# The last batch's tail rows are stored in two transfers instead of four

## The chip, the cores and the metric

The kernel runs on one core of a Trainium2 chip. The core has TensorE (PE in the profile), VectorE (DVE), ScalarE (ACT), GpSimd (POOL) and SyncE (SP), and 16 DMA engines that move data between the chip's memory and the core. A transfer is issued by an instruction on SP, ACT or POOL and then runs by itself. The metric is the device time of one execution in microseconds (us); shorter is better.

## The reference, cut to what matters

Eight batches of 576 rows go through sliding-window attention with 8 heads of 64, and then through a token mix and a channel mix:

```python
scores = scale * np.matmul(q, k.transpose(0, 1, 3, 2))     # 8 batches, 8 heads, 576 x 64
scores = np.where(mask, scores + bias[None], -1000000000.0) # window of 128, slope per head
attn = np.exp(scores - np.max(scores, axis=-1, keepdims=True))
x = np.matmul(attn / np.sum(attn, axis=-1, keepdims=True), v)   # -> 8 x 576 x 512
...
h = np.maximum(xt @ w_tok1, 0.0) @ w_tok2                   # token mix, 576 -> 256 -> 576
u = x + h.transpose(0, 2, 1)
h2 = np.maximum(u @ w_ch1, 0.0) @ w_ch2                     # channel mix, 512 -> 1536 -> 512
return (u + h2).astype(np.float32)                          # 8 x 576 x 512
```

## The kernel before, in words

The 576 rows of a batch are four blocks of 128 rows and a tail of 64. Two batches form a pair, and their two tails share one block: batch `2 * pr` in partitions 0 to 63, batch `2 * pr + 1` in partitions 64 to 127. The code calls this block `TAIL`. It is worked on with the second batch of the pair, so the output rows of the last tail block belong to batches 6 and 7 and are computed with batch 7, the last one.

The whole program is first written down as a list of operations with costs and ranks (`plan.op`), a planner (`Plan.run`) simulates them with those costs and settles the order of each engine, and `Plan.emit` writes the instructions in that order. Each operation holds a small function that issues its instructions when it is emitted. The planner's costs don't come from the instructions but are given by hand: the store of a tail block is planned as an operation of SP with cost 550.

For each batch, `side` computes attention and token mix, and `main` the channel mix. The first channel product is in `main` and its helpers; the second, of the four full blocks, is in `second` (lines 1160 to 1256), where the 512 x 512 results are formed by seven products of quarter size, whose sums are added in VectorE (L1202) and stored as quarters of 2 blocks x 128 rows x 256 columns (L1214). The last of these quarters in the last batch is formed by `last_product` in two blocks (matmuls L1263, add L1267); its two stores go out on SP and on ACT (L1270).

The tail block's second product is at the end of `main`: 12 matmuls (L1133), an add of the residual in VectorE (L1140), and a store (L1150). In the last batch it is cut into two column halves of 256 (`cuts`), each with matmuls, add and store of its own, and its stores go out on SP (`q_` is `nc.sync`). The outputs wait in a ring of six buffers, `ob` (named raw and ob in the profile). At the end of the program SP waits until the transfers have landed (L1350).

The order of SP's stores at the end of the program is: one quarter of L1214; the first column half of the tail; two quarters of L1214; the second column half of the tail; the L1270 store of one block. ACT issues the other L1270 store. A store in DRAM terms: the rows of `out` are 512 floats, of which a store of 256 columns writes 1 KB each; a batch is 576 rows.

Of the kernel before, what the change touches and what calls it, by code (L numbers as in the profile page):

```python
# [382 lines left out]
def kernel(  # L383
# [16 lines left out]
    P = nc.NUM_PARTITIONS  # L400
    B, H, S, D = q.shape
# [4 lines left out]
    NC = S // P  # L406
    R = S - NC * P
    NB = 2 * NC + 1
    TAIL = 2 * NC
# [24 lines left out]
    def bank(choice=ONE):  # L434
        return plan.buf("ps", choice)
# [581 lines left out]
    def main(b, rank):  # L1017
        pr, half = b // 2, b % 2
# [5 lines left out]
        if b == 0:  # L1024
            first = [bank() for _ in range(PIECES)]
            for blk in blocks:
                for t, ct in enumerate(first):
                    def go(t=t, ct=ct, blk=blk):
                        for cb in range(NCB):
                            pe_.matmul(ct()[:, blk * P : (blk + 1) * P], lhsT=WC1[:, cb, t * P : (t + 1) * P],  # L1030
                                       rhs=uT()[:, cb, blk * P : (blk + 1) * P],
                                       start=cb == 0, stop=cb == NCB - 1)
# [89 lines left out]
        for blk in blocks:  # L1122
            cuts = [slice(0, DM)]
            if b == B - 1 and blk == blocks[-1]:
                cuts = [slice(0, DM // 2), slice(DM // 2, DM)]
            for cols in cuts:
                o2 = bank()
                n = cols.stop - cols.start
                for g in range(NHT // 3):
                    def go(blk=blk, g=g, o2=o2, cols=cols):  # L1130
                        for t in range(3 * g, 3 * g + 3):
                            l = r2t()[:, t, :] if blk == TAIL else r2()[:, t, (blk % NC) * P : (blk % NC + 1) * P]
                            pe_.matmul(o2()[:, cols], lhsT=l, rhs=WC2[:, t, cols], start=t == 0, stop=t == NHT - 1)  # L1133

                    rk = rank(648)
                    rd = [(r2t, g * 3 // 4), (r2t, (g * 3 + 2) // 4)] if blk == TAIL else [(r2, t) for t in range(3 * g, 3 * g + 3)]
                    plan.op("PE", 649 * n / DM, go, rk, reads=rd, needs=lc2[3 * g : 3 * g + 3],
                            **({"makes": o2} if g == 0 else {"adds": o2}))
                ob = plan.buf("ob")
                plan.op("DVE", 160 + 530 * n / DM, lambda blk=blk, o2=o2, ob=ob, cols=cols: dve_.tensor_tensor(  # L1140
                    out=ob()[:, cols], in0=o2()[:, cols], in1=ub()[:, blk, cols], op=ALU.add), rk, makes=ob, uses=[o2],
                    reads=[(ub, blk)])

                late = b >= FROM_P and blk not in blocks[-2:] or FROM_P <= b < B - 1
                q_ = nc.gpsimd if late else nc.sync

                def store(blk=blk, ob=ob, cols=cols, q_=q_):
                    if blk == TAIL:
                        for i in range(2):
                            q_.dma_start(out=out[2 * pr + i, NC * P : S, cols], in_=ob()[i * R : (i + 1) * R, cols])  # L1150
                    else:
                        q_.dma_start(out=out[b, (blk % NC) * P : (blk % NC + 1) * P, cols], in_=ob()[:, cols])

                if late:
                    plan.dma(store, P, -1, uses=ob)
                else:
                    plan.op("SP", 550, store, rk, uses=[ob])
# [197 lines left out]
```

## Time and profile before

| what | value |
|---|---|
| timed runs | 277.51, 278.48, 278.57 us; median 278.48 |
| the profiled execution's own time | 277.36 us |
| its span | 275.6 us, at a granted TensorE clock of 1.0 |
| TensorE busy | 268.4 us (97%) |
| VectorE busy | 210.3 us (76%) |
| bytes moved by DMA | 38.71 MB |

The span runs from the first to the last instruction of the profiled execution; the execution's own time is a little longer. A row of the timeline gives start, length, engine, line and operation (output <- input), and in brackets how long the engine had been idle and what ended that. The letters SPq and ACTq mark instructions that issue a transfer: their length is that of the issue, not of the transfer. The DMA view gives the packets of each queue, the time they took as a share of 16 engines' time in the stretch asked for, and, for each line that issues, the median time from issue to landing. q1 is the queue of SP's transfers, q10 that of ACT's, q0 that of GpSimd's; q8 and q14 fetch instructions. A table by stretches has columns for stretch, length, busy time of PE, PEld, DVE, ACT and POOL with the number of instructions, the granted clock, the mean busy share of the 16 DMA engines, and GB/s.

### The profile page before, as it was taken

How to read it: one execution, taken by the hardware profiler on the slowest of the kernel's cores; microseconds unless marked ns; L12 is line 12 of the kernel's file. 1: busy time of each engine (PE TensorE's matmuls, PEld its weight loads, DVE VectorE, ACT ScalarE, POOL GpSimd, SP SyncE). 2: the span in 40 equal slices, each digit the busy share in tenths (PEclk: the TensorE clock that was granted, in tenths of full speed). 3: DMA queues.
4: the chain of work that ended last, by engine and by line, in shares of the span. 5: the costliest groups of instructions: out<-in, count | busy, mean ns of one | idle time of the engine just before them, and what ended most of it. 6: DMA issues, size and time to landing. Idle time of an engine off the chain costs nothing.

```text
span 275.6 us, 6968 instructions
## 1 busy us (share of the span) xinstructions
PE 268.4 (97%) x2790; PEld 180.8 (66%) x2824; DVE 210.3 (76%) x496; ACT 139.1 (50%) x239; POOL 114.0 (41%) x144
## 2 busy tenths in 40 slices
PE   8999999999999999999999999999999999999994
PEld 4665655676676556585658655576676655599983
DVE  7596799987898379956979468763998459967983
ACT  5475893426940388109950187116960089106560
POOL 8898747940454039700891009600462410021000
PEclk9999999999999999999999999999999999999999
DMA  8999999999899899979999859999599760043014
GB/s 156 154 165 178 179 200 183 155 129 210 127 107 130 176 233 142 152 120 193 189 149 148 199 146 95 135 158 242 68 99 126 195 132 0 2 113 137 1 49 145
DMA packets 167553, 38.71 MB, mean 140 GB/s; under 512 B 155808, under 2 KB 166688, under 8 KB 167520
## 3 DMA queue, kind: packets, MB, share of 16 engines
q0 software_dynamic: 114032, 19.77, 91.8%
q1 hardware_dynamic: 51264, 17.83, 33.4%
q10 hardware_dynamic: 2224, 0.66, 1.2%
q8 instruction: 22, 0.36, 0.5%
q14 instruction: 11, 0.09, 0.1%
HBM read 35.85 MB, written 9.44 MB: 164 GB/s over the span
## 4 chain that ended last, share of the span: by engine, by line
PE 81%; DMA 6%; DVE 5%; POOL 4%; issue 2%; SPq 1%; POOLq 0%
PE ps L1234 25%; PE ps L1045 24%; PE ps L760 6%; PE ps L693 5%; DMA qk<-in_k_dram 5%; PE ps L805 4%; PE ps L848 4%; PE ps L1088 4%; PE ps L967 3%; PE ps L1133 3%; DVE pe L726 2%; POOL qk L530 2%; POOL v L530 1%; DMA uT<-ub 1%; PE ps L815 1%
## 5 line engine op out<-in xcount | busy, mean ns | idle before, releaser
L1045 PE MATMUL ps<-uT,WC 128*128 128x512 bf16 x306 | 77.9, 379 | 1.3 <-DMA uT<-ub 0.2
L716 ACT ACTIVATE pe<-ps 128x1024 bf16<-128x1024 f32 (+1 forms) x76 | 63.4, 890 | 19.1 <-PE ps L693 18.8
L530 POOL DMA_DIRECT2D v<-in_v_dram x40 | 34.1, 858 | 91.8 <-PE ps L760 88.6
L1051 ACT ACTIVATE r<-ps 128x512 bf16<-128x512 f32 x77 | 45.0, 604 | 51.4 <-PE ps L1045 49.3
L1045 PEld LDWEIGHTS <-WC 128*128 128x128 bf16 x328 | 29.1, 98 | 29.3 <-issue 0.9
L726 DVE TENSOR_TENSOR pe<-pe,mask 128x1024 bf16<-128x1024 bf16 (+1 forms) x64 | 38.7, 609 | 12.0 <-ACT pe L716 11.5
L1234 PEld LDWEIGHTS <-r 128*128 128x128 bf16 x372 | 36.1, 98 | 7.3
L530 POOL DMA_DIRECT2D qk<-in_k_dram x38 | 33.0, 876 | 4.6 <-DMA WC<-in_moe_w_ch_dram 2.4
L530 POOL DMA_DIRECT2D qk<-in_q_dram x38 | 32.7, 866 | 1.7 <-PE ps L1234 0.7
L1234 PEld LDWEIGHTS <-s 128*128 128x128 bf16 x288 | 27.4, 98 | 6.0 <-issue 2.0
L776 DVE TENSOR_TENSOR xb<-ps,rt 128x256 bf16<-128x256 f32 (+1 forms) x72 | 28.9, 417 | 0.8
L760 PEld LDWEIGHTS <-pe 128*128 128x128 bf16 (+1 forms) x560 | 22.6, 98 | 9.1 <-DVE pe L726 1.3
L760 PE MATMUL ps<-v,pe 128*128 128x65 bf16 (+1 forms) x560 | 26.9, 194 | 0.3
L1234 PE MATMUL ps<-WC,r 128*128 128x256 bf16 x192 | 25.4, 273 | 0.0
L1234 PE MATMUL ps<-WT,s 128*128 128x256 bf16 x192 | 24.8, 273 | 0.0
L866 DVE TENSOR_TENSOR ub<-ps,xb 128x512 bf16<-128x512 f32 x34 | 21.3, 683 | 2.5 <-PE ps L848 2.5
L1234 PE MATMUL ps<-WT,r 128*128 128x256 bf16 x180 | 22.3, 273 | 0.0
L693 PEld LDWEIGHTS <-qkT 64*128 64x128 bf16 x560 | 14.8, 94 | 10.7 <-issue 8.2
L1202 DVE TENSOR_TENSOR raw<-ps,ub 128x512 f32<-128x512 f32 x22 | 15.0, 686 | 8.1 <-PE ps L1234 8.1
L693 PE MATMUL ps<-qkT 64*128 64x128 bf16 (+1 forms) x304 | 19.5, 216 | 0.0
L1093 ACT ACTIVATE r2t<-ps 128x512 bf16<-128x512 f32 x12 | 7.2, 600 | 22.9 <-PE ps L1088 22.7
L773 DVE RECIPROCAL rt<-ps 128x4 f32<-128x4 f32 (+1 forms) x76 | 12.6, 176 | 7.3 <-PE ps L760 6.9
(101 smaller groups left out, 348.1 us busy)
## 6 DMA issues: line engine op xcount, KB each, us to landing
out_dram<-raw SPq DMA_DIRECT2D x18, 256.0 KB, 2.8
v<-in_v_dram POOLq DMA_DIRECT2D x32, 128.0 KB, 5.1
qk<-in_k_dram POOLq DMA_DIRECT2D x30, 128.0 KB, 5.5
qk<-in_q_dram POOLq DMA_DIRECT2D x30, 128.0 KB, 5.1
WC<-in_moe_w_ch_dram POOLq DMA_DIRECT2D x8, 384.0 KB, 9.4
out_dram<-ob SPq DMA_DIRECT2D x5, 256.0 KB, 2.6
out_dram<-ob POOLq DMA_DIRECT2D x4, 256.0 KB, 2.7
out_dram<-raw POOLq DMA_DIRECT2D x4, 256.0 KB, 2.9
```

Of the source, the lines that this page charges most:

```text
L530: nc.gpsimd.dma_start(out=to()[p0 : p0 + n, :, :], in_=rows(src, b, s0, n))
L693: pe_.matmul(wide(e)[:, i, kind, a:z], lhsT=ts[kb]()[e * D : (e + 1) * D, NHP + i, :], rhs=ts[blk]()[e * D : (e + 1) * D, i, a:z], start=n ...
L716: act_.activation(out=pb()[:, e, :, lo:, c0:c1_], in_=wide(e)[:, :, lo:, c0:c1_], func=ACT.Exp, scale=scale)
L726: dve_.tensor_tensor(out=o, in0=o, in1=heads(mk, es), op=ALU.mult)
L760: pe_.matmul(view()[a:z, at, i, :], lhsT=pb()[:, e, i, kind, a:z], rhs=vb()[:, h, 0 : D + 1], start=m == 0, stop=m == len(mms) - 1, skip_g ...
L773: dve_.reciprocal(out=rt()[r0:r1_, 0:n, :, :], in_=view()[r0:r1_, :, :, D : D + 1])
L776: dve_.tensor_tensor(out=x4(), in0=view()[r0:r1_, :, :, 0:D], in1=rt()[r0:r1_, 0:n, :, :].broadcast_to([r1_ - r0, n, 4, D]), op=ALU.mult)
L866: plan.op("DVE", 690, lambda blk=blk, ht=ht, hs=hs: dve_.tensor_tensor(out=ub()[:, blk, :], in0=ht()[:, hs], in1=xb()[:, blk, :], op=ALU.a ...
L1045: pe_.matmul(ct()[:, :], lhsT=WC1[:, cb, t * P : (t + 1) * P], rhs=uT()[:, cb, :], start=cb == 0, stop=cb == NCB - 1)
L1051: plan.op("ACT", 600, lambda t=t, ct=ct: act_.activation(out=r2()[:, t, :], in_=ct()[:, :], func=ACT.Relu), rk, part=(r2, t), uses=[ct], o ...
L1202: dve_.tensor_tensor(out=v, in0=both(bk), in1=src, op=ALU.add)
L1234: pe_.matmul(of(bk, c), lhsT=l(t, c), rhs=w(t), start=first, stop=g == 1 and t == HK - 1, skip_group_check=True)
```

## The change

In the last batch, each column half of the tail block is stored by one transfer that covers both batches' 64 rows, instead of by one transfer for each batch. The source is all 128 partitions of the buffer; the destination takes 64 rows in each of two batches. The four transfers of the last tail block become two. The tails of the other pairs are stored as before, and the planner's cost of the store is not changed.

```diff
@@ -1145,7 +1145,9 @@
                 q_ = nc.gpsimd if late else nc.sync
 
                 def store(blk=blk, ob=ob, cols=cols, q_=q_):
-                    if blk == TAIL:
+                    if blk == TAIL and b == B - 1:
+                        q_.dma_start(out=out[2 * pr : 2 * pr + 2, NC * P : S, cols], in_=ob()[:, cols])
+                    elif blk == TAIL:
                         for i in range(2):
                             q_.dma_start(out=out[2 * pr + i, NC * P : S, cols], in_=ob()[i * R : (i + 1) * R, cols])
                     else:
```

Lines behind the change are two higher in the changed kernel: the new transfer is L1149, the two transfers of the other pairs L1152, and L1214, L1267, L1270 and L1350 become L1216, L1269, L1272 and L1352.

## The prediction

> **What bounds the kernel now.** I read the page's first lines, then the end of the chain that ended last, then the last 10 us in order of time: the change touches only stores issued there.
>
> ```profile
> span 275.6 us, 6968 instructions
> PE 268.4 (97%) x2790; PEld 180.8 (66%) x2824; DVE 210.3 (76%) x496; ACT 139.1 (50%) x239; POOL 114.0 (41%) x144
> PE 81%; DMA 6%; DVE 5%; POOL 4%; issue 2%; SPq 1%; POOLq 0%
> ...
> 270.31 1.32 PE ps L1263 x12
> 271.63 0.02 issue
> 271.66 0.42 DVE raw L1267
> ```
>
> TensorE is busy 97% of the span and makes up most of the chain. None of its work changes. The chain's last link is the VectorE add at 271.66, which ends at 272.08; the span ends at 275.6. So 3.5 us of the span come behind all computing, and they are stores. The timeline shows who issues them (SPq and ACTq rows: start, length of the issue):
>
> ```profile
> 266.75 0.42 DVE L1140 TENSOR_TENSOR ob<-ps,ub 128x256 f32<-128x256 f32 x1 [0.27 <-PE ps L1133]
> ...
> 267.24 1.12 SPq L1150 DMA_DIRECT2D out_dram<-ob  x2
> ...
> 268.06 0.69 DVE L1202 TENSOR_TENSOR raw<-ps,raw 128x512 f32<-128x512 f32 x1 [0.35 <-PE ps L1234]
> ...
> 268.77 1.69 SPq L1214 DMA_DIRECT2D out_dram<-raw  x2
> ...
> 270.35 0.42 DVE L1140 TENSOR_TENSOR ob<-ps,ub 128x256 f32<-128x256 f32 x1 [0.29 <-PE ps L1133]
> 270.84 1.11 SPq L1150 DMA_DIRECT2D out_dram<-ob  x2
> 271.00 0.42 DVE L1267 TENSOR_TENSOR raw<-ps,ub 128x256 f32<-128x256 f32 x1 [0.23 <-PE ps L1263]
> 271.66 0.42 DVE L1267 TENSOR_TENSOR raw<-ps,ub 128x256 f32<-128x256 f32 x1 [0.23 <-PE ps L1263]
> 272.04 0.56 SPq L1270 DMA_DIRECT2D out_dram<-raw  x1
> 272.12 0.36 ACTq L1270 DMA_DIRECT2D out_dram<-raw  x1
> ```
>
> The pairs at 267.24 and 270.84 (L1150) are the four transfers of the change. SP issues the last store of its own at 272.04, though its data were ready at 271.42: it stood behind the second pair. ACT's last store waits for its own add only. The DMA view of the stretch 262 to 276 gives issue to landing (last column), and the list of SP's waits what the end waits for:
>
> ```profile
> out_dram<-ob SPq DMA_DIRECT2D x4, 64.0 KB, 2.1
> out_dram<-raw SPq DMA_DIRECT2D x1, 128.0 KB, 2.2
> out_dram<-raw ACTq DMA_DIRECT2D x1, 128.0 KB, 1.8
> SPq L1350 <- DMA out_dram<-raw: 1.6, 1, 1.6
> ```
>
> SP's last store lands at 272.04 + 2.2 = 274.24, ACT's at 272.12 + 1.8 = 273.92. The end waits for the later one, and 275.6 - 274.24 = 1.36 us of ending follow. Stretches of 0.2 us show when bytes flow (last two columns: mean busy share of the 16 DMA engines, GB/s):
>
> ```profile
> 268.20:268.40 0.20, 0.20 (x4) 0.18 (x2) 0.20 (x1) 0.00 (x0) 0.00 (x0) 1.00 0.08 20
> 268.40:268.60 0.20, 0.20 (x4) 0.18 (x2) 0.20 (x1) 0.00 (x0) 0.00 (x0) 1.00 0.77 195
> ...
> 269.60:269.80 0.20, 0.20 (x4) 0.18 (x2) 0.20 (x1) 0.00 (x0) 0.00 (x0) 1.00 0.48 169
> ...
> 270.80:271.00 0.20, 0.20 (x4) 0.18 (x2) 0.00 (x0) 0.00 (x0) 0.00 (x0) 1.00 0.07 26
> 271.00:271.20 0.20, 0.20 (x4) 0.18 (x3) 0.20 (x1) 0.00 (x0) 0.00 (x0) 1.00 0.88 302
> ...
> 272.00:272.20 0.20, 0.00 (x0) 0.00 (x0) 0.08 (x1) 0.00 (x0) 0.00 (x0) 1.00 0.79 220
> ...
> 273.60:273.80 0.20, 0.00 (x0) 0.00 (x0) 0.00 (x0) 0.00 (x0) 0.00 (x0) 1.00 0.91 302
> 273.80:274.00 0.20, 0.00 (x0) 0.00 (x0) 0.00 (x0) 0.00 (x0) 0.00 (x0) 1.00 0.09 26
> ```
>
> First bytes of the first tail pair flow at about 268.35, 1.1 us behind its issue; of the two L1214 stores at about 269.7 and 270.95; of the second pair at about 271.95; the last byte flows at about 273.85. Each store is a short burst on all sixteen engines, with gaps between.
>
> **The change, part by part.** *Issues.* Two of SP's issues go, at the lengths of the first row:
>
> ```profile
> L1150 SPq DMA_DIRECT2D out_dram<-ob x6: 472/548/589, 158.3 to 271.4; - x6
> ...
> L1214 SPq DMA_DIRECT2D out_dram<-raw x18: 372/478/576, 57.2 to 270.1; - x18
> ```
>
> One issue fewer in the first pair is worth nothing: SP's next store (268.77) waits for an add that ends at 268.06 + 0.69. One fewer in the second frees SP at about 271.4, so its last store goes out at about 271.46 instead of 272.04 and lands near 273.7. Then ACT's, at 273.92, is last. The gain is 274.24 - 273.92 = 0.3 us, if nothing else changes. The new issue has three dimensions, as L1214's have, and those take 0.37 to 0.58 us; I take 0.55. Were it over 1.1 us, the gain would be gone.
>
> *Order and queues.* Planned costs are untouched, so every engine's instructions keep their order; no buffer of these stores is used again, so nobody waits for them but the end. SP's next issue waits for no transfer of the new pair. The other pairs of batches keep two transfers. Cost: none.
>
> *How the transfer is dealt out.* This is the term that decides. In all transfers of the kernel before, both sides begin with 64 or 128 rows at one stride: L1214's store puts the 128 partitions ahead of its two blocks, L1150's stores are 64 rows. The new destination begins with a count of 2, the batches, 576 rows apart, and then 64 rows; the source is 128 partitions at one stride. A cut along the first dimension of both sides can only make two shares, of 64 rows each. Sixteen shares would need a cut inside the second dimension on one side and inside the first on the other. No transfer in the trace asks for that, so no row prices it; the ends are two shares and sixteen. I take two, because each transfer the trace does show can be cut along its first dimension. The Trainium skill says the same ("DMA: Bandwidth & Descriptors", "Why a DMA increments its semaphore by 16 and not by 1"): the number of engines is the largest up to 16 that divides the slowest dimension of both sides, here 2; the trace, with sixteen throughout, agrees but doesn't test it. The same page's "Rules for kernel authors" speaks for the change: two transfers to disjoint partition halves should be one of 128 partitions. By that rule alone the sum is the -0.3 us above.
>
> *What two shares cost.* Each of two DMA engines moves 64 rows of 1 KB for each new transfer, and its part of every other store. DMA view by stretch, 264.8 to 267 (one L1214 store), 268.2 to 268.9 (one 64 KB store), 271.5 to 273 (a lone instruction packet on one engine, 0.09 MB in 11 such packets over the run, some 8 KB):
>
> ```profile
> q1 hardware_dynamic: 264, 0.26, 34.8%
> ...
> q1 hardware_dynamic: 80, 0.07, 36.9%
> ...
> q14 instruction: 1, 0.01, 1.3%
> q14 instruction: 11, 0.09, 0.1%
> ```
>
> A packet's price: 0.348 x 2.2 us x 16 / 264 = 46.4 ns; 0.369 x 0.7 x 16 / 80 = 51.7 ns, completions among them; and for a lone engine 0.013 x 1.5 x 16 = 0.31 us for 8 KB, 39 ns a KB. I take 46.4, the row of the same rows of 1 KB in long bursts, and keep 39 and 51.7 as the ends. The Trainium skill ("Advanced Engine Details and Errata", "Clock Domains") gives 42 to 43 ns for an unobstructed 1 KiB descriptor; by it the sum below would be +2.2 us, an estimate.
>
> On such an engine stand: first tail transfer 64 + 1 completion, two L1214 stores 16 + 1 each (256 rows over 16 engines), second tail transfer 65, the last two stores 8 + 1 each: 65 + 34 + 65 + 18 = 182 packets. At 46.4 ns the first runs from 268.35 to 271.37, beyond the 269.7 at which the next store's bytes come, and so on: the engine never runs dry again (the second tail transfer, there at 271.95, is reached at 272.95). The work ends at 268.35 + 182 x 0.0464 = 276.8, against 273.85: +2.95 us. That swallows the 0.3 us of the issue. At 39 ns: 268.35 + 7.1 = 275.45, +1.6; at 51.7 ns: 277.75, +3.9.
>
> **Sum.** +2.9 us on the profiled execution, whose own time is 277.36 (span 275.6): 280.3. The three timed runs are 277.51 to 278.57, median 278.48, 1.1 above the profiled one; the middle of the four is 278.0. I add the 2.9 to that: **280.9 us**.
>
> **The rivals.** *Sixteen shares anyway.* If the transfer is dealt out like the others, the stores stay bursts and only the issue counts: -0.3 us, 277.7, no change that can be told (under 0.5%, 1.4 us, is about what a measurement of this kernel can't tell from none). For it: all the stores shown used all engines. Against it: none had such a form. This is the case on the other side. It decides from four shares on: an engine then carries 33 + 17 + 17 packets, is idle again before 271.95, and ends 33 + 18 packets later, at 274.3, or +0.5 us.
> *Two shares, but cheap.* Two engines alone needn't share their way with fourteen others. At 39 ns it is +1.6 us, 279.6; below 38 ns (182 x 0.038 = 6.9) it falls under +1.4, and the change can't be told. For it: the lone packet. Against it: one packet of 8 KB has less overhead than eight of 1 KB.
> *A longer issue.* SP's new issue eats the time of the two it replaces, with sixteen shares: +-0, 278.0. Against it: L1214's issues of three dimensions, under 0.58 us.
>
> **How the numbers follow.** Two shares at 39 to 51.7 ns: 0.78. Two shares under 38 ns: 0.03. Sixteen shares: 0.14. Longer issue: 0.03. Something that gains over 0.5%: 0.02, since SP's whole second pair is worth 0.3 us. So slower 0.79, same 0.19, faster 0.02. The forecast's own range is 279.6 to 282.5 (278.57 + 3.9). The sixteen-share case is over 0.1 and the forecast's tails are uncertain, so the range reaches down to it: 277.7 to 282.5.
>
> **What would show it.** Right: SPq shows one L1149 issue at about 267.2 and one at 270.8 with the last store at about 271.5; their landing is 4 us or more instead of 2.1; behind 268.4 the busy share of the DMA engines lies near 2/16 = 0.12 for most of the time, up to about 276.8, where the last packets move at under 50 GB/s; the last landing and the span come 2.9 us later, the computing ends at 272.1 as before. The completions tell the shares too. In the stretch 262 to 276 the small packets are nine transfers by sixteen engines:
>
> ```profile
> DMA packets 1426, 1.34 MB, mean 95 GB/s; under 512 B 144, under 2 KB 1424, under 8 KB 1424
> ```
>
> After the change, sixteen shares would leave 7 x 16 = 112 and two shares 5 x 16 + 2 x 2 = 84, if each engine taking part sends one. Wrong: bursts of share 0.7 to 1.0 behind the new issues and landings near 2.1 us (sixteen shares), or a low share that ends by 275 (cheap packets).

## The result, and the profile after

The changed kernel takes 280.26 us (median of 6 runs, 279.71 to 280.81) against 277.78 us for the kernel before (median of 6 runs, three of them those shown above). The ratio is 1.0088, with a 95% interval of 1.0063 to 1.0114: slower by 2.5 us, beyond the half per cent that this measurement can tell. The profiled execution took 280.46 us, its span is 278.7 us.

From run to run the computing ends some tenths of a us earlier or later. A distance that doesn't depend on that is the one from the end of the last VectorE add to the end of the span; below it is called the tail of the span. Before, it was 275.6 - 272.08 = 3.52 us. These are the issues and the last adds of the changed kernel, from its timeline (start, length, engine, line):

```profile
span 278.7 us, 6966 instructions
...
267.41 0.42 DVE L1140 TENSOR_TENSOR ob<-ps,ub 128x256 f32<-128x256 f32 x1 [0.26 <-PE ps L1133]
267.90 0.63 SPq L1149 DMA_DIRECT2D out_dram<-ob  x1
269.44 1.69 SPq L1216 DMA_DIRECT2D out_dram<-raw  x2
271.50 0.53 SPq L1149 DMA_DIRECT2D out_dram<-ob  x1
271.67 0.42 DVE L1269 TENSOR_TENSOR raw<-ps,ub 128x256 f32<-128x256 f32 x1 [0.23 <-PE ps L1265]
272.13 0.58 SPq L1272 DMA_DIRECT2D out_dram<-raw  x1
272.33 0.42 DVE L1269 TENSOR_TENSOR raw<-ps,ub 128x256 f32<-128x256 f32 x1 [0.23 <-PE ps L1265]
272.78 0.37 ACTq L1272 DMA_DIRECT2D out_dram<-raw  x1
```

The last add ends at 272.75, 0.67 later than in the profile before. The change touches only stores, and the other kernels below end it anywhere from 271.69 to 272.59, so I take this for the run's own difference. The tail of the span is 278.7 - 272.75 = 5.95 us, 2.43 longer. SP's last store now leaves at 272.13, right behind its own add (272.09). The issue that was saved did come off SP. But see what happens to the stores. This is the DMA view of the stretch 262 to 280, issue to landing in the last column (the new transfers show no landing):

```profile
DMA packets 1366, 1.34 MB, mean 74 GB/s; under 512 B 84, under 2 KB 1364, under 8 KB 1364
...
out_dram<-raw SPq DMA_DIRECT2D x3, 256.0 KB, 3.5
out_dram<-ob SPq DMA_DIRECT2D x2, 128.0 KB
out_dram<-raw SPq DMA_DIRECT2D x1, 128.0 KB, 5.6
out_dram<-raw ACTq DMA_DIRECT2D x1, 128.0 KB, 4.7
```

The small packets are 84, down from 144: five transfers with sixteen completions and two with two. The last two stores land 5.6 and 4.7 us behind their issue instead of 2.2 and 1.8, so the last landing is 272.13 + 5.6 = 277.73. Stretches of 0.2 us (last columns: granted clock, busy share of the 16 DMA engines, GB/s):

```profile
269.00:269.20 0.20, 0.20 (x5) 0.18 (x3) 0.20 (x1) 0.00 (x0) 0.00 (x0) 1.00 0.07 20
...
269.80:270.00 0.20, 0.20 (x4) 0.18 (x3) 0.08 (x2) 0.00 (x0) 0.00 (x0) 1.00 0.14 51
270.00:270.20 0.20, 0.20 (x4) 0.18 (x3) 0.17 (x1) 0.00 (x0) 0.00 (x0) 1.00 0.14 46
...
271.80:272.00 0.20, 0.20 (x4) 0.19 (x2) 0.20 (x1) 0.00 (x0) 0.00 (x0) 1.00 1.02 338
...
274.00:274.20 0.20, 0.00 (x0) 0.00 (x0) 0.00 (x0) 0.00 (x0) 0.00 (x0) 1.00 0.59 82
...
275.80:276.00 0.20, 0.00 (x0) 0.00 (x0) 0.00 (x0) 0.00 (x0) 0.00 (x0) 0.50 0.12 41
276.00:276.20 0.20, 0.00 (x0) 0.00 (x0) 0.00 (x0) 0.00 (x0) 0.00 (x0) 0.50 0.14 51
...
277.00:277.20 0.20, 0.00 (x0) 0.00 (x0) 0.00 (x0) 0.00 (x0) 0.00 (x0) 0.50 0.13 46
277.20:277.40 0.20, 0.00 (x0) 0.00 (x0) 0.00 (x0) 0.00 (x0) 0.00 (x0) 0.50 0.05 15
```

The first new transfer flows from about 269.1, at first at 20 GB/s, then at a share of 0.14, that is 2 of 16 engines, and some 48 GB/s. For the last 1.4 us two engines alone are still at work. The last byte flows at about 277.25, 4.50 us behind the last add, against 273.85 - 272.08 = 1.77 before. (The clock of 0.50 stands in rows in which TensorE has no matmul left, x0; it brings the mean clock down to 0.992 and holds up no matmul.)

### The profile page after: what moved, and what is told of

The parts are those of the page before. It is cut to its first block, busy times and chain, and to the rows that moved or that the text cites. A ratio compares the mean times of both kernels' runs of the same rounds, so it can differ in the third digit from the quotient of the medians.

```text
span 278.7 us, 6966 instructions
## 1 busy us (share of the span) xinstructions
PE 268.2 (96%) x2790; PEld 180.2 (65%) x2824; DVE 210.2 (75%) x496; ACT 139.1 (50%) x239; POOL 113.9 (41%) x144
## 4 chain that ended last, share of the span: by engine, by line
PE 85%; DMA 5%; DVE 4%; POOL 3%; issue 2%; POOLq 0%
PE ps L1236 26%; PE ps L1045 24%; PE ps L760 6%; PE ps L693 5%; PE ps L848 5%; PE ps L805 4%; PE ps L1133 4%; PE ps L1088 4%; PE ps L967 3%; DMA qk<-in_k_dram 3%; DMA W<-in_moe_w_tok_dram 2%; DVE pe L726 2%; POOL v L530 1%; POOL qk L530 1%; PE ps L815 1%
```

## The experiments

Each is the changed kernel with other stores of the last tail block. The diffs show the two lines of the change and what stands in their place. The tail of the span is told for each, and the ratio of its time to that of the kernel before.

| kernel | last add ends, span | tail of the span, us | last byte behind the last add, us | ratio, 95% interval |
|---|---|---|---|---|
| before | 272.08, 275.6 | 3.52 | 1.77 | |
| changed | 272.75, 278.7 | 5.95 | 4.50 | 1.0088, 1.0063 to 1.0114 |
| first half joined | 271.99, 275.5 | 3.51 | 2.1 | 0.9991, 0.9977 to 1.0005 |
| second half joined | 271.69, 277.2 | 5.51 | 3.8 | 1.0090, 1.0064 to 1.0115 |
| four of 62 rows | 272.27, 278.5 | 6.23 | 4.6 | 1.0112, 1.0085 to 1.0140 |
| four of 57 rows | 272.03, 276.0 | 3.97 | 2.3 | 1.0020, 1.0004 to 1.0036 |
| four of 60 rows | 272.28, 275.6 | 3.32 | 1.6 | 0.9997, 0.9985 to 1.0008 |
| joined, GpSimd | 272.40, 279.8 | 7.40 | 5.1 | 1.0146, 1.0129 to 1.0163 |
| no tail stores | 272.38, 275.2 | 2.82 | 1.4 | 0.9978, 0.9962 to 0.9993 |
| SP and ACT | 272.49, 275.8 | 3.31 | 1.6 | 0.9993, 0.9979 to 1.0006 |
| first pair on GpSimd | 272.11, 275.2 | 3.09 | | 0.9980, 0.9970 to 0.9990 |
| the same, and ACT | 272.59, 275.7 | 3.11 | | 0.9975, 0.9962 to 0.9988 |

### One half joined at a time

```diff
-                    if blk == TAIL and b == B - 1:
+                    if blk == TAIL and b == B - 1 and cols.start == 0:
```

> Only the first column half of the tail is stored in one transfer; the second keeps two. Measure: the time from the end of the last VectorE add to the end of the span (before 3.52 us, changed kernel 5.95). Theory (a joined transfer runs on two DMA engines, and these two are a queue, 45 ns a packet): the first transfer and the two block stores behind it occupy them until 0.7 us after the last add, then only 10 + 18 packets are left: last byte 2.0 us after the add against 1.77 before, so 3.5 to 3.9 us, and the time within 0.4 us of before. Rival (each joined transfer has a cost of its own, about half of the 2.4 us): 4.7 us, 1.2 us slower.

The tail of the span was 3.51 us and the time can't be told from before. The other half (`cols.start > 0`):

> Only the second column half is stored in one transfer. Theory (two DMA engines as a queue): its 65 packets begin at once when its bytes come, about 0.1 us before the end of the last add, and the 18 packets of the last two stores follow: last byte 83 x 45 ns = 3.7 us behind that, 3.6 us after the add, so 5.0 to 5.4 us from the add to the end, 1.5 to 1.9 us slower than before. Rival (a cost of its own for each joined transfer): 4.7 us, as with the first half alone.

The tail of the span was 5.51 us, 2.0 longer than before: somewhat over the 5.0 to 5.4 that the queue gives, and far from the 4.7 of the rival. So a joined transfer has no cost of its own. The first half's is as long as the second's, but its first bytes come 3.6 us before the end of the last add, and by the end its two engines have nearly caught up. The stretches at the end of the kernel with only the first half joined show how closely that ends, and those with the second half joined that it doesn't:

```profile
273.60:273.80 0.20, 0.00 (x0) 0.00 (x0) 0.00 (x0) 0.00 (x0) 0.00 (x0) 1.00 0.66 220
273.80:274.00 0.20, 0.00 (x0) 0.00 (x0) 0.00 (x0) 0.00 (x0) 0.00 (x0) 0.51 0.13 46
274.00:274.20 0.20, 0.00 (x0) 0.00 (x0) 0.00 (x0) 0.00 (x0) 0.00 (x0) 0.50 0.08 26
```

```profile
274.60:274.80 0.20, 0.00 (x0) 0.00 (x0) 0.00 (x0) 0.00 (x0) 0.00 (x0) 0.50 0.15 51
...
275.20:275.40 0.20, 0.00 (x0) 0.00 (x0) 0.00 (x0) 0.00 (x0) 0.00 (x0) 0.50 0.13 46
275.40:275.60 0.20, 0.00 (x0) 0.00 (x0) 0.00 (x0) 0.00 (x0) 0.00 (x0) 0.50 0.05 15
```

With the first half joined two engines are left alone for about 0.3 us, with the second for over 1 us. The 0.0 of the first half is not quite free. These are the issue and the landing of the store that lands last, first with the first half joined, then with the second:

```profile
272.00 0.65 SPq L1272 DMA_DIRECT2D out_dram<-raw  x1
out_dram<-raw SPq DMA_DIRECT2D x1, 128.0 KB, 2.5
```

```profile
271.73 0.37 ACTq L1272 DMA_DIRECT2D out_dram<-raw  x1
out_dram<-raw ACTq DMA_DIRECT2D x1, 128.0 KB, 4.1
```

The first lands at 274.50, 2.51 us behind the last add, 0.35 later than before (2.16); the span then ends 1.00 us behind it instead of 1.36, which hides the loss ("The ending", below). The second lands at 275.83, 4.14 behind the add, 1.98 later than before, with an ending of 1.37. So up to the last landing the halves lose 0.35 and 1.98 us, and both together 2.82 (277.73 - 272.75 = 4.98). The 0.5 us beyond the sum fits a queue that is still full when the second transfer comes and passes its delay on; no run measures that apart.

### Two engines without joining anything

The joined store differs from the four in its number of transfers, in its form, and in the number of engines. Against the kernel before, this run changes the engines alone, by the number of rows:

```diff
-                        q_.dma_start(out=out[2 * pr : 2 * pr + 2, NC * P : S, cols], in_=ob()[:, cols])
+                        for i in range(2):
+                            q_.dma_start(out=out[2 * pr + i, NC * P : NC * P + 62, cols], in_=ob()[i * R : i * R + 62, cols])
```

> Four transfers as in the kernel before, in its plain form of two dimensions, but each of 62 rows instead of 64: the last two rows of each tail are left out of the store in the last batch. Theory (the number of engines is the largest up to 16 that divides the first dimension of both sides): 62 = 2 x 31, so two engines again, 32 packets a transfer: 4 x 32 + 34 + 18 = 180 packets from the first byte on, and 5.7 to 6.3 us from the last add to the end, 2.2 to 2.8 us slower than before, though nothing is joined; small packets in the last 14 us: 4 x 2 + 5 x 16 = 88. Rival (the joined form with three dimensions is what is slow, or the fewer issues): as before, 3.5 us, 144 small packets or nearly.

It moves less than the kernel before and takes 6.23 us from the last add to the end, longer than the changed kernel: its last byte comes 0.1 us later, and its ending behind the last landing is 1.30 us (278.5 - 277.20) instead of 0.97. The DMA view of the stretch 262 to 280 has the 88 small packets, and a stretch near the end the two engines:

```profile
DMA packets 1362, 1.33 MB, mean 74 GB/s; under 512 B 88, under 2 KB 1360, under 8 KB 1360
```

```profile
276.40:276.60 0.20, 0.00 (x0) 0.00 (x0) 0.00 (x0) 0.00 (x0) 0.00 (x0) 0.50 0.15 51
```

So neither the joining nor the third dimension is what costs: the number of engines is. Two more row counts tell how it is chosen (the diff is the same with 60 and 57):

> Four transfers of 60 rows instead of 64 in the last batch; the last four rows of each tail are not stored. A control for the run with 62 rows. Theory (the number of engines is the largest up to 16 that divides the row count): 15 engines, 4 rows each, so as the kernel before: 3.3 to 3.7 us from the end of the last VectorE add to the end of the span, time within 0.4 us of before, 4 x 15 + 5 x 16 = 140 small packets in the last 14 us. Rival (any count that isn't 64 or 128 is slow): 6.2 us as with 62 rows, 2.5 us slower.

> Four transfers of 57 rows; the last seven rows of each tail are not stored. Theory (57 = 3 x 19, so three engines, 19 + 1 packets a transfer at 45 ns, these engines a queue): the queue has almost caught up when the second pair's bytes come, 0.1 us before the end of the last add; then 40 + 18 packets, last byte 2.5 us after the add against 1.77 before; 3.9 to 4.4 us from the add to the end, 0.4 to 0.9 us slower than before, 4 x 3 + 5 x 16 = 92 small packets. Rival (the loss goes with the bytes per engine alone, 19 rows against 32 a transfer, so 19/32 of the 2.7 us that 62 rows cost): 1.6 us slower, 5.1 us.

```profile
DMA packets 1406, 1.32 MB, mean 73 GB/s; under 512 B 140, under 2 KB 1404, under 8 KB 1404
```

```profile
DMA packets 1346, 1.31 MB, mean 73 GB/s; under 512 B 92, under 2 KB 1344, under 8 KB 1344
...
273.80:274.00 0.20, 0.00 (x0) 0.00 (x0) 0.00 (x0) 0.00 (x0) 0.00 (x0) 1.00 0.20 72
```

60 rows: 140 small packets, 15 engines, nothing lost (the tail of the span is even 0.2 us shorter; its second pair of issues takes SP 0.80 us instead of 1.11). 57 rows: 92 small packets, a share of 0.20 (three of sixteen) at 72 GB/s, 0.45 us on the tail of the span and 0.2% on the time, as the queue gives and far from the 1.6 us that go by bytes alone. Four counts, 57, 60, 62 and the joined 2 x 64, fall on 3, 15, 2 and 2 engines: the largest number up to 16 that divides the first dimension of both sides. This is the rule of the Trainium skill ("DMA: Bandwidth & Descriptors", "Why a DMA increments its semaphore by 16 and not by 1"), and these runs test it where the kernel before couldn't. That both sides count isn't tested: a rule that goes by the destination alone would give the same four numbers here.

### Another queue

```diff
-                        q_.dma_start(out=out[2 * pr : 2 * pr + 2, NC * P : S, cols], in_=ob()[:, cols])
+                        nc.gpsimd.dma_start(out=out[2 * pr : 2 * pr + 2, NC * P : S, cols], in_=ob()[:, cols])
```

> The two joined transfers are issued by GpSimd instead of SP. Theory A (GpSimd deals them out by the same rule): two engines again, 5.9 to 6.5 us from the last add to the end, as slow as the changed kernel or a little slower, since GpSimd's issue is longer. Theory B (only SP's and ACT's queues deal by it): sixteen engines, and SP's last store no longer waits behind a tail store: 3.1 to 3.6 us, no slower than before.

Two engines again, and slower than expected: 7.40 us. At the end a share of 0.13 moves 51 GB/s. The small packets don't tell the shares in this kernel: 480 of the 560 are beyond the 80 of the five block stores, and GpSimd's 256 KB travel in 64 packets of over 2 KB.

```profile
DMA packets 1650, 1.34 MB, mean 75 GB/s; under 512 B 560, under 2 KB 1584, under 8 KB 1648
...
276.80:277.00 0.20, 0.00 (x0) 0.00 (x0) 0.00 (x0) 0.00 (x0) 0.00 (x0) 0.50 0.13 51
277.20:277.40 0.20, 0.00 (x0) 0.00 (x0) 0.00 (x0) 0.00 (x0) 0.00 (x0) 0.50 0.12 46
```

The last byte is 0.6 us later than in the changed kernel, GpSimd's first bytes being later by about as much; the rest of the loss lies behind the last byte (2.3 us against 1.45), where SP's waits for TensorE's sequencer (PEq) take 1.2 us instead of 0.7; what else is in it stays open. So the dealing isn't a matter of SP's queue.

### What there was to gain

```diff
-                        q_.dma_start(out=out[2 * pr : 2 * pr + 2, NC * P : S, cols], in_=ob()[:, cols])
+                        pass
```

> The last batch's tail rows are not stored at all. It bounds what any rearrangement of these stores can bring. Theory (only one of SP's issues stands on the path, and ACT's store is next to last): SP's last store goes out at the end of its own add, ACT's store lands last, 3.1 to 3.3 us from the last add to the end, 0.2 to 0.5 us faster than before. Rival (the four transfers cost the end more than one issue, by their bytes): 3.0 us or less, 0.6 us or more faster.

```profile
272.42 0.36 ACTq L1272 DMA_DIRECT2D out_dram<-raw  x1
```

```profile
out_dram<-raw SPq DMA_DIRECT2D x1, 128.0 KB, 2.1
out_dram<-raw ACTq DMA_DIRECT2D x1, 128.0 KB, 1.7
```

These are ACT's last issue in the timeline of this kernel, and the landings of the last two stores in its DMA view. Without any tail store the tail of the span is 2.82 us, 0.70 less than before, and the time 0.6 us shorter (ratio 0.9978). That is the rival's number rather than the theory's: beside the issue there was another gain. ACT's store lands last, 1.7 us behind its issue at 272.42, so at 274.12, 1.74 behind the last add, 0.42 sooner than SP's before (274.24 - 272.08 = 2.16). The other 0.28 us lie behind the last landing, where the span ends after 1.08 us instead of 1.36. The gain up to the landing is within the theory's 0.2 to 0.5 us; what goes beyond it is the ending, so that the four transfers' bytes cost anything, as the rival has it, isn't shown.

Taking the one issue off SP without two engines:

```diff
-                        q_.dma_start(out=out[2 * pr : 2 * pr + 2, NC * P : S, cols], in_=ob()[:, cols])
+                        for i in range(2):
+                            (nc.sync, nc.scalar)[i].dma_start(out=out[2 * pr + i, NC * P : S, cols],
+                                                              in_=ob()[i * R : (i + 1) * R, cols])
```

> Four transfers of 64 rows as in the kernel before, on sixteen engines each, but of each pair one is issued by SP and one by ACT, which has nothing else to do there. It takes the one issue off SP that the joined transfer was to take off, without dealing the bytes to two engines. Theory: SP's last store goes out 0.55 us sooner, ACT's lands last, 3.1 to 3.4 us from the last add to the end, 0.1 to 0.5 us faster than before, at the limit of what can be told. Rival (SP's and ACT's issues hold each other up): 3.5 us or more, no gain.

The tail of the span was 3.31 us, 0.2 shorter; the time, 0.9993 with an interval of 0.9979 to 1.0006, shows no gain. SP's last store left right behind its add, but ACT's last landed 2.0 us behind its issue instead of 1.8:

```profile
272.53 0.37 ACTq L1274 DMA_DIRECT2D out_dram<-raw  x1
out_dram<-raw ACTq DMA_DIRECT2D x1, 128.0 KB, 2.0
```

That is 274.53, 2.04 behind the last add, 0.1 us sooner than before; the other 0.1 is the ending. The issue that the change was to save is worth 0.1 to 0.2 us here, less than these runs resolve.

### The ending

The distance from the last landing to the end of the span isn't the same in all these kernels. The transfers of SP and ACT take eight semaphores in turn, so two transfers more or fewer shift which semaphore the last one has. Two kernels test whether that matters; the first:

```diff
-                        q_.dma_start(out=out[2 * pr : 2 * pr + 2, NC * P : S, cols], in_=ob()[:, cols])
+                        for i in range(2):
+                            e_ = nc.gpsimd if cols.start == 0 else nc.sync
+                            e_.dma_start(out=out[2 * pr + i, NC * P : S, cols], in_=ob()[i * R : (i + 1) * R, cols])
```

> All four transfers of 64 rows stay, on sixteen engines, but the two of the first column half are issued by GpSimd, whose transfers count on semaphores of their own; the second half as in the kernel before. The transfers of SP and ACT take eight semaphores in turn, and at the end SP looks at these in a fixed order: with two transfers fewer in the turn, SP's last store moves from the first of the eight, behind which seven are still to be looked at, to the seventh. In the runs so far the span ends 1.36 and 1.37 us behind the last landing where that was on the first of the eight, 1.24 to 1.30 on the second, 1.08 on the sixth, 0.97 and 1.0 on the seventh and eighth. Theory (each semaphore still to be looked at costs some 50 ns at the end): last landing 2.2 us after the last add as before, ending 0.95 to 1.0 us behind it: 3.0 to 3.3 us from the add to the end against 3.52, 0.2 to 0.5 us faster. Rival (the length of the ending has another cause, and goes with the run): 3.5 us, no change.

In the second, the second pair has `(nc.sync, nc.scalar)[i]` in place of `nc.sync`:

> As the run with the first column half on GpSimd, and of the second half's two transfers one is issued by ACT, so that SP's last store goes out sooner. ACT's last store is then the last to land, on the eighth of the semaphores. Theory: last landing 1.8 to 2.0 us after the last add, ending 0.95 to 1.0 us behind it: 2.8 to 3.0 us from the add to the end, 0.5 to 0.7 us faster than before. Rival (no gain from the order of the semaphores): 3.3 us, 0.2 us faster at most, as the run with the stores split between SP and ACT alone.

Both are faster than the kernel before: 0.9980 (0.9970 to 0.9990) and 0.9975 (0.9962 to 0.9988), some 0.6 us, the best found here, and too little for a single run to tell. The first kernel's last stores, from its timeline and its DMA view:

```profile
272.09 0.59 SPq L1274 DMA_DIRECT2D out_dram<-raw  x1
272.15 0.37 ACTq L1274 DMA_DIRECT2D out_dram<-raw  x1
```

```profile
out_dram<-raw SPq DMA_DIRECT2D x1, 128.0 KB, 2.2
```

```profile
span 275.2 us, 7002 instructions
```

The last landing is at 274.29, 2.18 behind the last add as before, and the span ends 0.91 us later instead of 1.36. With the landing unchanged, the ending alone is shorter, as the order of the semaphores gives. The second kernel's last issue and its landing:

```profile
272.62 0.36 ACTq L1274 DMA_DIRECT2D out_dram<-raw  x1
```

```profile
out_dram<-raw ACTq DMA_DIRECT2D x1, 128.0 KB, 2.1
```

It did not add the 0.2 us hoped for: its ACT store landed 2.1 us behind its issue, at 274.72, again 2.13 behind the last add, and the tail of the span, 3.11 us, was more than the 2.8 to 3.0 expected. That first pair was also moved to another queue; that this in itself brings nothing is argued from the unchanged landing, not measured by itself.

The traces show SP going through the semaphores. These are its semaphore instructions behind the last landing, of the kernel before (stretch 274.2 to 274.75) and of the changed one (277.6 to 277.83), with their number, their lengths in ns, and the start of the first and the last:

```profile
L1350 SPq EVENT_SEMAPHORE  x8: 28/28/28, 274.3 to 274.7; - x8
```

```profile
L1352 SPq EVENT_SEMAPHORE  x2: 28/28/28, 277.7 to 277.8; - x2
```

Eight start within 0.4 us, some 60 ns from one to the next. Behind the landing of the changed kernel six fewer are left, about 0.36 us.

## Why the prediction was right

**Direction and size.** 280.9 us was forecast, 280.26 measured, in the range; +2.9 us against +2.5. The other 0.2 us are the base: 278.0 was taken for the kernel before, and its median came out at 277.78.

**The issues: right.** One new issue takes 0.63 and 0.53 us (0.55 assumed), and SP's last store leaves at 272.13, right behind its add. As forecast the gain is swallowed. Its worth by itself, 0.3 us, was on the high side: splitting the pair between SP and ACT gave 0.2 on the tail of the span, half of it up to the last landing.

**Two shares: right, and now shown.** The 84 completions and the share of 0.14 at 46 to 51 GB/s are what two shares were to leave. The choice rested on the form of the transfer, since no row could price it; the rows of 62, 60 and 57 show the same in plain stores.

**The price of a packet: nearly right.** The two engines move 182 packets from about 269.1 to 277.25, 45 ns each against 46.4 taken, the slow start included. In the last 1.4 us, where they are alone, 41 to 51 GB/s for two engines, 47 on the mean of seven stretches, make 43 ns for 1 KB. That agrees with the 42 to 43 ns of the Trainium skill ("Advanced Engine Details and Errata", "Clock Domains"). So the last byte came 2.73 us later behind the last add, not 2.95.

**The queue: right.** That the first transfer still holds up the second, and that the order of the work makes the loss, is borne out by the two halves: 0.35 and 1.98 us up to the last landing, and more than the sum for both. What the prediction did not say is that the first half alone would have cost next to nothing.

**The ending: the mis-sized term.** The prediction let 1.36 us follow the last landing, as before. It was 278.7 - 277.73 = 0.97. With two transfers fewer the last store had a later semaphore in the order that SP looks at, and two of SP's semaphore instructions were left behind its landing instead of eight. The sum as measured: +2.73 to the last byte, +0.1 from there to the landing (0.48 against 0.39), -0.39 behind it: +2.43 us.

**The rivals.** Sixteen shares anyway: fell with the 84 completions. Cheap packets: fell with 45 ns. A longer issue: fell with 0.53 us.

**Signs that were not as told.** The computing ended at 272.75 and not at 272.1. The landing of the new transfers can't be read, since their row shows none. Between the end of the first joined transfer and the last one's, the share was not 0.12 "for most of the time": the block stores run on all engines in between (share 1.02 at 271.80).

## What to carry to other kernels

Look at the first dimension of both sides before joining two stores: a joined transfer with a leading count of 2 runs on two DMA engines, and each following transfer on the same engines waits behind it; fewer transfers can then be slower ones. A long transfer on few engines costs little where its engines can nearly catch up before the end (0.35 us for the first half here), and most of its length where they can't (2.0 us for the second, whose 65 packets at 45 ns are 2.9 us). At the end of a program read the last stores as a queue per engine, and price the issue, the bytes and the ending apart.

## What the runs showed of the hardware that was not expected

The ending goes with the semaphore of the last landing, as far as these runs show it: 1.36 and 1.37 us behind it on the first of eight, 0.91 to 1.0 on the last two. These distances make some 50 to 75 ns for each that is still to be looked at (0.36 / 7, 0.45 / 6), and SP's rows some 60 ns. That SP looks at the semaphores in a fixed order is read from the program; no run changed the order alone.

While two engines are backed up, the engines that are busy move less each, by the mean of all of them. In the changed kernel at 274.00 a share of 0.59 moves 82 GB/s, 8.7 GB/s for a busy engine (82 / 0.59 / 16), where before a share of 0.91 at 273.60 moved 302, 20.7 each. It didn't set the end here, since the two engines had work throughout. Which engines are slowed, and by what, stays open.

The same joined transfer from GpSimd's queue also runs on two engines, and the stores of 60 and 62 rows are issued faster than those of 64 rows: a pair takes SP 0.80 and 0.68 us against 1.11. Why stays open.
